# A fused state-space and linear-attention kernel: the data load over two queues, cosines from ScalarE, PSUM reads on either engine, wider lag products, and a new instruction order

## The chip, the core and the metric

The kernel runs on one core of a Trainium2 chip. The time is device microseconds of one execution. Five executions of the kernel before gave 340.03 to 342.0 us, with a median of 341.09 us. Besides, one execution was taken by the hardware profiler, and every row below is from it.

## What is computed

The input x is 2048 positions by 512 channels. The output is `g * a + (1 - g) * b`, where g is a sigmoid gate per position.

Branch a is a long convolution (a state-space model). Each channel d has a kernel K of 2048 lags, the real part of a sum over 128 states n, and `y = irfft(rfft(K) * rfft(x))` per channel, plus a skip term:

```
P = exp(dt * A * l)              # complex, for every channel, state, lag l
K = einsum("dn,dnl,dn->dl", C, P, dt * B).real
```

Branch b is linear attention with 32 heads of 16 features. Queries and keys pass a small matrix and a softmax of both signs, `phi = [softmax(p), softmax(-p)]`; keys and values are summed to one matrix per head, queries are multiplied with it and divided by their sum, and the result is multiplied by `wo`.

## The kernel before

**Plan.** Nothing is scheduled by a compiler. Every piece of work is recorded with `P.add(engine, cost, function, deps, ...)` (class `Plan`, L92). `Plan.schedule` (L161) then places the pieces one by one by their written costs, priorities and buffer rings, and the pieces are emitted in that order. Each engine works through its own queue in order. `TIES` (L97) are seeds of random changes to the priorities; together with the costs they fix the order. A piece may name several engines with a cost each, and the planner takes the one that ends first: the helper `evict` (inside `keys_and_spectrum`) does so for copies from PSUM.

**Loads and tables (`prepare`).** ScalarE's queue issues six parameter loads (L356). SP's queue issues UD (x in 16 pieces of 128 KB, `load_ud` L1426), the weights (`load_w`) and log_dt (`load_ld`, tiles ldc and ld). Tables of sines and cosines for the transform (TB, TI, TJ, W) come from `trig`: POOL writes a ramp into the buffer tgc, VectorE turns it into an integer angle (L397, L398), ScalarE takes the sine. TB has three planes: sine, cosine (both by `trig`) and the negated sine (L414, VectorE). After a table load, a chain over VectorE and ScalarE makes C and D (Ctab, Dtab), from which the powers of the state-space model are made. It starts with dt = exp(log_dt) (tile dtc) and with copies of the transposed B (L491, L492). In between, TensorE transposes x (xT) and makes the spectrum of x (psA, XAu, psB, XU). The gate is `gps`, `gz`, `gT`, and in row form `zps`, `zrow`.

**Keys.** For 16 tiles of positions: pk (TensorE), Ek (two exponentials), Zk (sum), vp, vr (product), kvp (accumulated). Then KVbd, KVT and Mw combine keys, values and wo.

**Queries.** Four blocks: pq, Eq (exponentials), zs (sums), a chain lnZ, den, apm, then aexp and the product Eq (L1046), and bps (16 of them), written to DRAM as bSd.

**Convolution.** For 8 heads of 64 channels, in two chunks each: exponentials E and cosines cs of args (ScalarE; each head needs a change of the activation table and back), the products A (L1102 to L1104) and R (L1116, L1117) on VectorE, kps on TensorE, its copy KD, psA, its copy XA. A transform (`transform`) per two heads, the last two heads singly: psB, copy XK, products t with the spectrum of x, psz, copy Zr, a turn through DRAM (Zd, ZT), psy, the sum bS, four stores. The very last transform takes another way without DRAM (L1276, Z, L1319), and splits its stores over two queues. The eight copies KD, and XA, XK, Zr, are on ScalarE.

R is made one lag part at a time:

```
lo = -x if o == 1 else x                              # ns, L1114
R[:, o, :, 32:64] = E[:, :, 32:64] * x                # L1116, 1024 elements
R[:, o, :, 0:32]  = E[:, :, 0:32] * lo[:, :, ::-1]    # L1117, 1024 elements
```

Of the kernel before, what the change touches and what calls it, by code (L numbers as in the profile page):

```python
# [91 lines left out]
class Plan:  # L92
# [3 lines left out]
    SLACK = 0.0  # L96
    TIES = ((52116, 4, 0.1), (24065, 0.5, 0.1), (41416, 1, 0.1), (45222, 1, 0.05), (61293, 2, 0.02), (71070, 0.5, 0.1),  # L97
            (31770, 1, 0.02), (57566, 0.5, 0.1), (45785, 1, 0.02), (57629, 8, 0.02), (66806, 2, 0.02), (29666, 2, 0.02),
            (61795, 2, 0.1), (13489, 2, 0.05), (14232, 0.5, 0.05), (54586, 0.5, 0.02), (70633, 2, 0.1), (38980, 0.5, 0.05),
            (69021, 4, 0.02), (29818, 2, 0.02), (36790, 2, 0.05), (49753, 1, 0.05), (54801, 2, 0.05), (64205, 4, 0.02),  # L100
            (37415, 2, 0.05), (26019, 0.5, 0.02), (40764, 1, 0.02), (81418, 0.5, 0.02), (60489, 0.5, 0.02), (18238, 0.5, 0.02),
            (76206, 0.5, 0.05), (96767, 4, 0.05), (53026, 0.5, 0.02), (71470, 1, 0.02), (92667, 0.5, 0.05), (83600, 4, 0.02),
            (94213, 4, 0.02), (56684, 4, 0.02), (33149, 8, 0.02), (31465, 2, 0.05), (85177, 2, 0.02), (77498, 1, 0.02),
            (99872, 0.5, 0.02), (5344, 1, 0.05), (71573, 1, 0.02), (46960, 4, 0.02), (29130, 8, 0.02), (30878, 1, 0.05),
            (24195, 2, 0.02), (71220, 0.5, 0.05))
# [27 lines left out]
    def dma(self, busy, late, fn, deps=(), take=(), drop=(), rw=("", ""), move=0.0):  # L133

        i = self.add("SP", busy, fn, deps, take, rw=rw)
        m = self.add("D", move, lambda: None, [i]) if move else i
        n = self.add("W", late, lambda: None, [m], (), drop)
        n.issue = i
        for k in rw[0].split():
            if self.keys[k][1] and i in self.keys[k][1]:  # L140
                self.keys[k][1].append(n)
        for k in rw[1].split():
            self.keys[k] = (n, [])
        return n
# [16 lines left out]
    def schedule(self, bias, slack=0.0):  # L161
# [7 lines left out]
        while left:  # L169
            cand = []  # L170
            for n in left:
                best_e = None
                for e, c in (n.eng if isinstance(n.eng, list) else [(n.eng, n.cost)]):
                    t = free.get(e, 0.0) if e not in "WX" else 0.0
                    for d in n.deps:
                        x = d.end + (self.LAT if d.at != e else 0.0)
                        if x > t:
                            t = x
                    if best_e is None or t + c < best_e[0]:
                        best_e = (t + c, t, e, c)  # L180
                _, t, e, c = best_e
                if n.tab is not None and n.tab != state:
                    continue
                ok, ring = True, None
                for r in n.take:
                    if isinstance(r, str) and r not in self.dyn:
                        continue
                    alt = []
                    for q in ([r] if isinstance(r, str) else r):
                        m = taken[q] - self.k[q]  # L190
                        if q in shut or (m >= 0 and m not in given[q]):
                            continue
                        alt.append((max(t, given[q][m].end + self.LAT if m >= 0 else since[q].end if q in since else 0.0), -self.k[q] + taken[q], q))
                    if not alt:
                        ok = False
                        break
                    t, _, ring = min(alt)
                if ok:
                    cand.append((t, -n.prio - bias[n.i], n.i, n, e, c, ring))
# [37 lines left out]
    def bias(self, seeds):  # L237
        import random
        b = [0.0] * len(self.nodes)
        for s, amp, share in seeds:  # L240
            r = random.Random(s)
            for i in range(len(b)):
# [92 lines left out]
def prepare(P, tc, nc, g, evict, psum):  # L335
# [22 lines left out]
    P.dma(1.1, 3.0, lambda: g.load_ld(), rw=("", "ldc ldb"))  # L358
    P.add("W", 7.0, lambda: None, rw=("raw0", "raw"))
    for tg in range(4):  # L360
        P.dma(4.2, 3.0, lambda tg=tg: g.load_ud(tg), rw=("", f"ud{tg}"))
    P.dma(2.5, 5.5, lambda: g.load_w(), rw=("", "wsm wqk"))
# [4 lines left out]
    def first():  # L367
# [5 lines left out]
        nc.gpsimd.memset(F.mpi[:], -PI_S)  # L373
        F.v = [g.ctmp.tile([128, 2048], I32, name=f"tgv{i}") for i in range(2)]
# [37 lines left out]
    for i, o in ((0, SIN), (1, COS)):  # L412
        trig(lambda i=i: tb(i), 2048, p63, lambda o=o: o, 1, [[2, 32], [128, 64]], f"TB{i}")
    V(1.6, lambda: nc.vector.tensor_scalar(out=tb(2), in0=tb(0), scalar1=-1.0, scalar2=None, op0=ALU.mult), r="TB0", w="TB2")  # L414
# [230 lines left out]
def keys_and_spectrum(P, tc, nc, g, psum):  # L645
# [147 lines left out]
    for s2 in range(8):  # L793
        K = Bag()
        red = []
        for u in range(2):
# [20 lines left out]
            a = P.add("PE", 1.05, pk, [a] if u else [sp, lnexp] + xt + kp, take=["bk"] + ([] if u else ["Ek", "Zk", "vr"]))  # L817
# [9 lines left out]
        for u in range(2):  # L827
# [25 lines left out]
            a = P.add("PE", 1.05, pv, [a], take=["bk"], rw=("wqk", ""))  # L853
            c = P.add("DVE", 1.36, sc, [a, l], drop=["psum"])
            kv = [P.add("PE", 0.45, kn, [c] + kv, drop=(["Ek", "vr"] if u else []))]
# [4 lines left out]
def plan_tables(P, nc, g, psum, h, prev, start=()):  # L860
# [4 lines left out]
    for i in range(2):  # L865
        G = 2 * h + i
        for b2 in range(2):
# [14 lines left out]
            a = P.add("PE", 0.62, pe, [T.first] if b2 else list(start), take=[psq] + (["E"] if b2 == 0 else []))  # L882
# [3 lines left out]
    for i in range(2):  # L886
# [14 lines left out]
        ra.append((P.add("PE", 0.62, pe, T.nE + list(start), take=[psq, "cs"]), sc))  # L901
# [7 lines left out]
def queries_and_convolution(P, tc, nc, g, psum, sh, sp, sl, kv, bank, evict):  # L909
# [3 lines left out]
    W1 = fc.W1[:].rearrange("p r i d -> p (r i d)")  # L913

# [55 lines left out]
    for b in range(4):  # L970
        Q = Bag()
        eq = []
        for m in range(4):
# [14 lines left out]
            a = P.add("PE", 1.0, pq, [sh, sp] + ([a] if m else []), take=["bk"] + ([] if m else ["r8"]))  # L988
# [13 lines left out]
        z = P.add("PE", 2.4, zz, eq + [sk], take=["acc", "nrm"])  # L1002
# [29 lines left out]
        for i in range(4):  # L1032
# [39 lines left out]
            pb = P.add("PE", 2.1, pbm, em + [pb] + mw, take=["bk", "bs"], drop=(["r8", "nrm"] if i == 3 else []))  # L1072
# [9 lines left out]
    def kgen(h, T, XA, new):  # L1082
# [4 lines left out]
        for cc in range(2):  # L1087
# [3 lines left out]
            def Cb(i, d0=d0):  # L1091
                return g.C[:, i, :, d0:d0 + 32].unsqueeze(2).to_broadcast([128, 4, 8, 32])

            def Db(i, d0=d0):
                return g.D[:, i, :, d0:d0 + 32].unsqueeze(1).to_broadcast([128, 4, 8, 32])

            def a_half(o, c=c, Cb=Cb, Db=Db):
# [3 lines left out]
                (i0, j0), (i1, j1), op = (((0, 0), (1, 1), ALU.add), ((0, 1), (1, 0), ALU.subtract))[o]  # L1101
                nc.vector.tensor_tensor(out=c.A[:, o], in0=Cb(i0), in1=Db(j0), op=ALU.mult)  # L1102
                nc.vector.tensor_tensor(out=tmp[:], in0=Cb(i1), in1=Db(j1), op=ALU.mult)  # L1103
                nc.vector.tensor_tensor(out=c.A[:, o], in0=c.A[:, o], in1=tmp[:], op=op)  # L1104

            def r_half(o, c=c, cc=cc):
                if o == 0:
                    c.R = g.rk.tile([128, 2, 32, 64], BF16, name="R")
                E = T.E[cc]
                x = T.cs[cc][:, o]  # L1110
                lo = x
                if o == 1:
                    ns = g.wk.tile([128, 32, 32], BF16, name="ns", tag="tmp", bufs=1)
                    nc.vector.tensor_scalar(out=ns[:], in0=x, scalar1=-1.0, scalar2=None, op0=ALU.mult)  # L1114
                    lo = ns[:]
                nc.vector.tensor_tensor(out=c.R[:, o, :, 32:64], in0=E[:, :, 32:64], in1=x, op=ALU.mult)  # L1116
                nc.vector.tensor_tensor(out=c.R[:, o, :, 0:32], in0=E[:, :, 0:32], in1=lo[:, :, ::-1], op=ALU.mult)  # L1117
                if o == 1:
                    T.E[cc] = T.cs[cc] = None
            a0 = P.add("DVE", 1.95, lambda f=a_half: f(0), [sk], take=["A"])  # L1120
            a1 = P.add("DVE", 1.95, lambda f=a_half: f(1), [a0])
            tdeps = [T.nE[2 * cc], T.nE[2 * cc + 1], T.nc[cc]] if T.nE else []
            r0 = P.add("DVE", 1.3, lambda f=r_half: f(0), tdeps + [sk], take=["R"])
            r1 = P.add("DVE", 1.65, lambda f=r_half: f(1), [r0], drop=["E", "cs"])
# [6 lines left out]
            kps.append(P.add("PE", 1.4, lambda f=kp: f(0), [a0, a1, r0, r1] + kps, take=([psq, "KD"] if cc == 0 else []), drop=["A", "R"]))  # L1131

        def kd():
            K.KD = g.wk.tile([128, 2, 4, 128], BF16, name="KD", bufs=1)
            nc.scalar.copy(out=K.KD[:], in_=K.ps[:].rearrange("p c g e t -> p c g (e t)"))
            K.ps = None
        d = P.add("ACT", 1.03, kd, kps, drop=["psum"])
        for cc in range(2):
# [12 lines left out]
            def ex(cc=cc, box=box):  # L1151
                slot = (0 if new else 2) + cc
                nc.scalar.copy(out=XA.t[:].rearrange("p r i (c d g) -> p (r i) c d g", d=4, g=4)[:, :, slot, :, :],
# [3 lines left out]
            K.done.append(P.add("ACT", 1.03, ex, [s], drop=["psum"]))  # L1157
# [21 lines left out]
    def transform(XA, ready, Q, off, nd, far, L, last):  # L1179
# [11 lines left out]
        for r0 in range(0, 32, ns):  # L1191
# [20 lines left out]
            def xk(box=box):  # L1212
                box.XK = g.fpool.tile([128, ns, nd], BF16, name="XK", tag="XK", bufs=2)
                nc.scalar.copy(out=box.XK[:].rearrange("p s (c e x) -> p (s c) e x", e=2, x=16),  # L1214
# [18 lines left out]
            x = P.add("ACT", 1.03, xk, [b], drop=["psum"])  # L1233
# [14 lines left out]
            def fe(box=box):  # L1248
                box.Z = g.fpool.tile([128, ns, nd], BF16, name="Zr", tag="Zr", bufs=2)
                nc.scalar.copy(out=box.Z[:], in_=box.ps[:])  # L1250
# [6 lines left out]
            zn.append(P.add("ACT", 1.03, fe, [z] + zn[-1:], drop=["psum"]))  # L1257
# [111 lines left out]
def full_kernel(tc, A_u, A_A_re, A_A_im, A_B_re, A_B_im, A_C_re, A_C_im, A_log_dt, A_Dskip,  # L1369
# [7 lines left out]
    with ExitStack() as ctx:  # L1377
# [48 lines left out]
        def load_ud(tg):  # L1426
            for dj in range(4):
                nc.sync.dma_start(out=g.UD[32 * dj:32 * dj + 32, 16 * tg:16 * tg + 16, :],  # L1428
# [130 lines left out]
```

The softmax here doesn't subtract the row's maximum and nothing guards it: scores larger than these inputs give would overflow.

## Time and profile before

| what | value |
|---|---|
| median of 5 runs | 341.09 us |
| profiled execution, its own time | 341.22 us |
| its span | 339.4 us |
| mean granted TensorE clock | 0.827 |
| TensorE, VectorE, ScalarE busy | 247.3, 279.4, 257.2 us |
| DMA | 24.62 MB in 58666 packets, 54145 of them under 512 B |
| first product of the table chain on VectorE (L455) starts | 26.04 us |
| first Ek starts | 80.22 us |
| first and last bps | 153.84 us, 219.4 us |
| last R ends | 305.2 us |

In the rows below, PE is TensorE, DVE is VectorE, ACT is ScalarE, SPq and ACTq are the queues on which DMAs are issued. A row of the timeline has start, duration, engine, line, operation, output and input, and in brackets how long the engine was idle before it and what ended that. A row of the windows has the stretch, and for each engine the busy time with the number of its instructions, then the granted clock, the share of the 16 DMA engines that was busy (transfers overlap, so it can be over 1) and GB/s.

### The profile page before, as it was taken

What the parts mean: (1) busy time and instruction counts of PE and PEld (TensorE: products, weight loads), DVE (VectorE), ACT (ScalarE), POOL (GpSimd) and SP (SyncE); (2) the same over time, 40 slices, a digit from 0 to 9 for tenths busy, and PEclk for the clock granted to TensorE, in tenths of its full rate; (3) what the DMA queues carried; (4) which work ended last, traced back from release to release, by engine and by line L of the source; (5) the groups of instructions that cost most, each with busy time, mean ns of one, the idle gap of its engine ahead of it and who ended that gap; (6) DMA issues with size and microseconds to landing.
All of it is one profiled execution on the core that took longest, in us unless ns stands there. A gap on an engine that the chain in (4) does not pass through costs nothing.

```text
span 339.4 us, 9785 instructions
## 1 busy us (share of the span) xinstructions
PE 247.3 (73%) x4290; PEld 145.8 (43%) x4320; DVE 279.4 (82%) x478; ACT 257.2 (76%) x332; POOL 12.2 (4%) x24
## 2 busy tenths in 40 slices
PE   0417675479998979569999998976776769978750
PEld 0405564355554424233544544444343534456530
DVE  8969999995897985896598897299999999895531
ACT  2847998896977557964976897899979998897200
POOL 5420010000000000000000000000000000000000
PEclk9955569556999978957999999996998985697985
DMA  9991600000000000000201011272176278768444
GB/s 144 249 151 37 150 3 0 2 0 2 2 3 2 4 0 2 2 1 17 49 15 34 17 33 31 46 179 90 64 181 130 68 187 185 191 186 172 113 79 80
DMA packets 58666, 24.62 MB, mean 73 GB/s; under 512 B 54145, under 2 KB 55297, under 8 KB 58113
## 3 DMA queue, kind: packets, MB, share of 16 engines
q1 hardware_dynamic: 54400, 23.10, 30.9%
q10 hardware_dynamic: 4224, 0.92, 1.9%
q8 instruction: 33, 0.54, 0.7%
q14 instruction: 9, 0.07, 0.1%
HBM read 11.42 MB, written 8.39 MB: 58 GB/s over the span
## 4 chain that ended last, share of the span: by engine, by line
DVE 39%; PE 37%; issue 7%; ACT 7%; SPq 5%; DMA 4%; ACTq 0%; DVEq 0%
PE bps L1056 7%; DVE A L1104 5%; DVE Atmp L1103 5%; DVE A L1102 5%; PE pk L803 5%; DVE R L1117 4%; PE pq L981 4%; PE vp L835 4%; SPq L1428 3%; PE args L876 3%; PE aexp L1041 2%; DVE R L1116 2%; PE kps L280 2%; DVE pt L493 2%; DVE t L1221 2%
## 5 line engine op out<-in xcount | busy, mean ns | idle before, releaser
L83 ACT ACTIVATE E<-args 128x1024 bf16<-128x1024 f32 x32 | 32.0, 1037 | 3.5 <-PE args L876 3.5
L1056 PE MATMUL bps<-Mw,Eq 128*128 128x512 bf16 x122 | 31.2, 394 | 1.7 <-DVE Eq L1046 1.1
L83 ACT ACTIVATE cs<-args 128x1024 bf16<-128x1024 f32 x32 | 30.8, 1032 | 0.1
L1046 DVE TENSOR_TENSOR Eq<-Eq,aexp 128x512 bf16<-128x512 bf16 x32 | 20.4, 682 | 10.2 <-PE aexp L1041 10.2
L681 PE MATMUL psA<-W,UD 128*64 128x256 bf16 x128 | 16.8, 420 | 16.1 <-DMA ldc<-in_A_log_dt_dram 5.5
L75 ACT ACT_TABLE_LOAD x20 | 25.7, 1283 | 1.1 <-PEq L1543 0.7
L1116 DVE TENSOR_TENSOR R<-E,cs 128x1024 bf16<-128x1024 bf16 x32 | 21.9, 686 | 4.3 <-PE kps L280 4.3
L876 PE MATMUL args<-selE,stat 64*128 64x512 bf16 x64 | 21.3, 446 | 5.2 <-ACT cs L83 2.9
L280 PE MATMUL kps<-R,A 128*32 128x64 bf16 x1024 | 18.8, 230 | 8.0 <-DVE A L1104 3.9
L815 DVE TENSOR_REDUCE Zk<-Ek 128x64 f32<-128x1024 bf16 x16 | 18.8, 1214 | 6.0 <-ACT Ek L83 5.9
L1104 DVE TENSOR_TENSOR A<-A,Atmp 128x1024 bf16<-128x1024 bf16 x32 | 22.1, 692 | 1.1
L1102 DVE TENSOR_TENSOR A<-Ctab,Dtab 128x1024 bf16<-128x1024 bf16 x32 | 21.9, 686 | 1.2 <-PE kps L280 1.2
L83 ACT ACTIVATE Ek<-pk 128x512 bf16<-128x512 f32 x32 | 16.8, 599 | 7.9 <-PE pk L803 7.9
L280 PEld LDWEIGHTS <-A 128*32 128x32 bf16 x1024 | 17.1, 152 | 11.8 <-issue 6.7
L1103 DVE TENSOR_TENSOR Atmp<-Ctab,Dtab 128x1024 bf16<-128x1024 bf16 x32 | 21.9, 685 | 0.0
L681 PEld LDWEIGHTS <-UD 128*64 128x64 bf16 x128 | 13.1, 207 | 19.5 <-issue 19.0
L1244 PE MATMUL psz<-t,TI 128*128 128x512 bf16 x50 | 17.8, 464 | 4.4 <-ACT cs L83 3.0
L595 PE MATMUL xps<-ident,UD 128*128 128x128 bf16 x64 | 7.2, 286 | 18.8 <-DMA Dcol_b<-in_A_Dskip_dram 10.9
L839 DVE TENSOR_TENSOR vr<-vp,vr 128x512 bf16<-128x512 f32 x32 | 19.6, 681 | 0.0
L83 ACT ACTIVATE Eq<-pq 128x512 bf16<-128x512 f32 x32 | 16.8, 612 | 3.5 <-PE pq L981 3.5
L1056 PEld LDWEIGHTS <-Eq 128*128 128x128 bf16 x128 | 12.0, 100 | 16.9 <-DVE Eq L1046 3.0
L1214 ACT CAST XK<-psB 128x1024 bf16<-128x1024 f32 x16 | 16.1, 1025 | 1.6 <-PE psB L1206 0.9
(195 smaller groups left out, 560.8 us busy)
## 6 DMA issues: line engine op xcount, KB each, us to landing
XUs<-XU SPq DMA_DIRECT2D x8, 512.0 KB, 6.7
Zd<-Zr SPq DMA_DIRECT2D x14, 256.0 KB, 4.5
ZT<-Zd SPq DMA_DIRECT2D x6, 512.0 KB, 5.6
UD<-in_A_u_dram SPq DMA_DIRECT2D x16, 128.0 KB, 5.3
bSd<-bs SPq DMA_DIRECT2D x16, 128.0 KB, 1.9
bS<-bSd SPq DMA_DIRECT2D x4, 512.0 KB, 7.9
out_dram<-bS SPq DMA_DIRECT2D x30, 64.0 KB, 2.4
wqk<-in_B_wqkv_dram SPq DMA_DIRECT2D x1, 1024.0 KB, 6.6
```

The source lines that it names most:

```text
L75: p = self.nc.scalar.preload_act_table_set(name)
L83: i = self.nc.scalar.activation(**kw)
L280: nc.tensor.matmul(kps[32 * dj:32 * dj + 32, g4, e, :], lhsT=A[:, ri, :, :, d].rearrange("p a b -> p (a b)"), rhs=R[:, ri, d, :], start=(r ...
L681: nc.tensor.matmul(box.ps[64 * e:64 * e + 64, i, :], lhsT=g.UD[:].rearrange("p t (e g) -> p g e t", e=2)[:, gw * h + 4 * g4 + i, e, :], rh ...
L839: nc.vector.tensor_tensor(out=K.v[:, u, sg, :, 0:32].rearrange("p m (h e) -> p m h e", e=16), in0=box.ps[:].rearrange("p (m h e) -> p m h ...
L876: nc.tensor.matmul(box.ps[:, 8 * j:8 * j + 8, :], lhsT=g.stat[0:64, G, :], rhs=g.selE[0:64, d0:d0 + 8, :], start=True, stop=True, tile_pos ...
L1046: nc.vector.tensor_tensor(out=e, in0=e, in1=box.ps[:], op=ALU.mult)
L1056: nc.tensor.matmul(box.ps[:], lhsT=Q.e[:, m, sg, 128 * i:128 * i + 128], rhs=g.Mw[:, 4 * sg + m, :], start=(k == 0), stop=False, skip_grou ...
L1102: nc.vector.tensor_tensor(out=c.A[:, o], in0=Cb(i0), in1=Db(j0), op=ALU.mult)
L1103: nc.vector.tensor_tensor(out=tmp[:], in0=Cb(i1), in1=Db(j1), op=ALU.mult)
L1104: nc.vector.tensor_tensor(out=c.A[:, o], in0=c.A[:, o], in1=tmp[:], op=op)
L1116: nc.vector.tensor_tensor(out=c.R[:, o, :, 32:64], in0=E[:, :, 32:64], in1=x, op=ALU.mult)
```

## The change

- `load_ud` may go on SP or on ScalarE's queue, as the planner chooses. In the built order, one of the four groups (four DMAs) is on ScalarE's, ahead of the first table. SP issues the weights first, then log_dt, then the other twelve pieces of UD.
- TB's cosine is made by ScalarE from the integer angle of the sine: an Abs into tgc, then a sine of it; the negated sine is a third activation. The second angle on VectorE and POOL and the negation L414 go.
- KD, XA, XK, Zr may be copied by ScalarE or VectorE; a new constant (LEAN, 0.6) is added to VectorE's end in that choice. In the built order VectorE has one XA and two XK; KVT, which had the choice before, is on ScalarE.
- R of both lag parts is one product of 2048 elements, twice per chunk, with the negation made in place between them.
- Some costs are changed, SLACK is 0.1, and TIES are 300 new seeds with ranges. The order is another one all over: the gate follows the keys, selE follows the last vr, lnZ and apm of the first block precede the first change of the activation table.

The core of the diff (TIES and the remaining costs left out):

```diff
-    P.dma(1.1, 3.0, lambda: g.load_ld(), rw=("", "ldc ldb"))
+    ld = P.dma(1.7, 3.0, lambda: g.load_ld(), rw=("", "ldc ldb")).issue
...
-        P.dma(4.2, 3.0, lambda tg=tg: g.load_ud(tg), rw=("", f"ud{tg}"))
-    P.dma(2.5, 5.5, lambda: g.load_w(), rw=("", "wsm wqk"))
+        P.dma(3.3, 2.5, lambda tg=tg: g.load_ud(tg, nc.scalar if P.cur.at == "ACT" else nc.sync), [ld], rw=("", f"ud{tg}"), eng=[("SP", 3.3), ("ACT", 3.4)], move=1.5)
+    P.dma(3.5, 5.5, lambda: g.load_w(), rw=("", "wsm wqk"), move=4.0)
...
-    for i, o in ((0, SIN), (1, COS)):
-        trig(lambda i=i: tb(i), 2048, p63, lambda o=o: o, 1, [[2, 32], [128, 64]], f"TB{i}")
-    V(1.6, lambda: nc.vector.tensor_scalar(out=tb(2), in0=tb(0), scalar1=-1.0, scalar2=None, op0=ALU.mult), r="TB0", w="TB2")
+    trig(lambda: tb(0), 2048, p63, lambda: SIN, 1, [[2, 32], [128, 64]], "TB0")
+    k0, v0, f0 = f"v{(nv[0] - 1) % 2}", (nv[0] - 1) % 2, 2.0 * PI_S / 8192.0
+    S(2.0, lambda: nc.scalar.activation(out=F.col[:], in_=F.v[v0][:], func=ACT.Abs, scale=f0, bias=F.mpi[:]), r=k0, w="col")
+    S(2.0, lambda: act(out=tb(1), in_=F.col[:], func=ACT.Sin, scale=-1.0, bias=HALF_PI), r="act col", w="TB1")
+    S(2.0, lambda: act(out=tb(2), in_=F.v[v0][:], func=ACT.Sin, scale=-f0, bias=F.ppi[:]), r="act " + k0, w="TB2")
...
+    def copy(out, in_):
+        if P.cur.at == "DVE":
+            nc.vector.tensor_copy(out=out, in_=in_)
+        else:
+            nc.scalar.copy(out=out, in_=in_)
...
-                nc.vector.tensor_tensor(out=c.R[:, o, :, 32:64], in0=E[:, :, 32:64], in1=x, op=ALU.mult)
-                nc.vector.tensor_tensor(out=c.R[:, o, :, 0:32], in0=E[:, :, 0:32], in1=lo[:, :, ::-1], op=ALU.mult)
...
+                    nc.vector.tensor_tensor(out=c.R[:, :, :, 32:64], in0=E[:, :, 32:64].unsqueeze(1).to_broadcast([128, 2, 32, 32]), in1=x[:], op=ALU.mult)
+                    nc.vector.tensor_scalar(out=x[:, 1], in0=x[:, 1], scalar1=-1.0, scalar2=None, op0=ALU.mult)
+                else:
+                    nc.vector.tensor_tensor(out=c.R[:, :, :, 0:32], in0=E[:, :, 0:32].unsqueeze(1).to_broadcast([128, 2, 32, 32]), in1=x[:, :, :, ::-1],
+                                            op=ALU.mult)
...
-            x = P.add("ACT", 1.03, xk, [b], drop=["psum"])
+            x = P.add([("ACT", 1.03), ("DVE", 1.24)], 1.03, xk, [b], drop=["psum"])
```

## The prediction

> **What bounds the kernel now.** I read the page's busy shares, then its slices, then windows of 20 us, because shares of a whole span mix stages.
>
> ```profile
> span 339.4 us, 9785 instructions
> PE 247.3 (73%) x4290; PEld 145.8 (43%) x4320; DVE 279.4 (82%) x478; ACT 257.2 (76%) x332; POOL 12.2 (4%) x24
> ...
> DMA  9991600000000000000201011272176278768444
> ```
>
> No engine is full over the span; the first three DMA slices are. The windows (engine busy, granted clock, DMA share, GB/s) show a stage with its own limit each time:
>
> ```profile
> 40.00:60.00 20.00, 12.17 (x185) 10.40 (x185) 19.65 (x34) 19.11 (x23) 0.95 (x1) 0.76 0.00 1
> ...
> 160.00:180.00 20.00, 19.79 (x225) 9.74 (x227) 16.20 (x28) 17.29 (x25) 0.00 (x0) 1.00 0.16 34
> 180.00:200.00 20.00, 19.43 (x311) 10.68 (x313) 17.91 (x31) 16.05 (x25) 0.00 (x0) 1.00 0.10 22
> ...
> 240.00:260.00 20.00, 12.37 (x262) 7.32 (x264) 19.76 (x34) 18.13 (x20) 0.00 (x0) 0.99 0.46 122
> ```
>
> From 26 to 76 us VectorE and ScalarE are both full (tables of the SSM kernel); from 155 to 219 TensorE is (queries, bps); from 221 to 305 VectorE is (products of the lags). What starts the first of these is in the timeline:
>
> ```profile
> 6.02 0.40 SPq L1433 DMA_DIRECT2D wc<-in_B_w_phi_dram  x1
> ...
> 9.88 11.03 SPq L1428 DMA_DIRECT2D UD<-in_A_u_dram  x12
> ...
> 20.96 0.71 SPq L1423 DMA_DIRECT2D ldc<-in_A_log_dt_dram  x1
> ...
> 25.80 0.21 ACT L83 ACTIVATE dtc<-ldc 128x4 f32<-128x4 bf16 x1 [2.13 <-DMA ldc<-in_A_log_dt_dram]
> ...
> 26.04 0.69 DVE L455 SCALAR_TENSOR_TENSOR pt<-Are,dtc 128x512 f32<-128x512 bf16 x1 [3.21 <-ACT dtc L83]
> ```
>
> log_dt is issued last, and VectorE waits 3.2 us for it. The SP queue's own waits say why issuing takes so long:
>
> ```profile
> SPq L1433 <- DMA Aim<-in_A_A_im_dram: 1.0, 1, 1.0
> ```
>
> wc has nothing to do with A_im: the built program gives every DMA one of eight semaphores in turn, and an issue waits until the transfer eight places earlier has landed.
>
> **Step 1, the start: +6.2 us.** The change moves ldc and ld ahead of UD, so that wait of 3.2 us goes. Next is late what ScalarE must do before its copies of B and C: it gains an Abs and two sines and loses one sine of 2048 (2.00 us each, so +4.0), while VectorE loses 1.28, 2.25 and 1.66 us. Four UD issues now stand on ScalarE's queue, ahead of all of that. In the built order they wait for Bim, Wv, ldc and the first UD that SP issues; that one stands behind ld, which waits for wqk. Params and wqk together are 1.8 MB; at the 181 to 381 GB/s of the windows around that time wqk lands near 9, ld is issued, UD at about 10, and lands 3.4 us later at the earliest (UD's landings: 3.4 to 7.2). Queued behind these waits are the Abs, the sines, an xT eviction and the table load; VectorE's products and TensorE's psA groups wait for those. So ScalarE is free for the Abs at about 13.4; the integers it needs are ready at about 9. Behind it come: Abs and cosine 4.05; on POOL the next ramp, which now waits for the cosine since both use one buffer (1.14), and the small ramp (1.17); VectorE's W, TI group 1.8 and the next integers 0.85; the third ramp 1.6 on POOL before masks and selectors (2.6); TJ and integers 2.0; the last sine 1.15, table load 1.28, copy 0.6, with gaps of 0.6: 18.8. VectorE's first product starts at 32.2 instead of 26.04. The bounds: +1.9 if nothing waits for landings, +12 if UD lands late. From there to the last table VectorE is busy 49.1 of 50.4 us and both orders put 10 evictions on it and 20 on ScalarE: the delay passes on whole. [...] With the DMA share at 1.4 from 4 to 24 us the data doesn't end earlier either.
>
> **Step 2, no gate between tables and keys: -2.3.** Before, the gate's 64 matmuls and two XU groups stand in TensorE's queue ahead of pk:
>
> ```profile
> 74.70 1.85 PE L763 MATMUL gps<-gw,xT 128*128 128x1 bf16 x64 [0.29 <-ACT XAu L662]
> ...
> 78.70 5.13 PE L803 MATMUL pk<-Wkp,xT 128*128 128x512 bf16 x15 [0.33 <-issue]
> ...
> 80.22 1.09 ACT L83 ACTIVATE Ek<-pk 128x512 bf16<-128x512 f32 x2 [0.80 <-PE pk L803]
> ```
>
> The last sine of the tables ended 6.5 us before that Ek. In the new order only two evictions (1.9), the table load (1.28) and one eviction (0.95) lie between: 4.2. Bounds 0 and -2.5.
>
> **Step 3, keys: -2.9.** selE (2.29), its helpers and zrow (0.68) leave VectorE's queue ahead of the last Zk and vr; it was full from 110 to 126. They reappear behind the last vr, where it waited 3.1 us for kvp anyway. TensorE's matmuls there differ by about nothing (gate and two groups in, 8 args and zps out). Bounds 0 and -4.
>
> **Step 4, keys to queries: +1.5, then -3.8.** KVT goes to ScalarE behind twelve Eq exponentials, and gate and zrow go between KVbd and Mw: +1.5 (0 to 3). From the last Mw (139.4) to the first bps (153.84) the old order has a table load, four cs and a table load (1.28, 3.77, 1.28) ahead of lnZ on ScalarE. The new one puts lnZ, den and apm ahead of them, behind five E (1.03) and three A groups (1.93) at most: 10.9 instead of 14.7. Bounds -1 and -6.
>
> **Step 5, queries: +3.** Between first and last bps the new order has 128 kps and 8 args more: 2 x 1.06 (64 kps took 1.06 at full clock) and 8 x 0.23 make 4.0. TensorE idled 2.3 us in that stretch, some of which covers it. Bounds 0 and +5.
>
> **Step 6, the VectorE stage.** Counted in both orders, what VectorE has left after the last Eq is the same: 20 groups of A, R for 10 chunks, 32 t, 8 bS. But before, it stood still first, its two R buffers full (R waited 4.3 for kps, in one wait); with one head more of kps done, that goes: -4.3 (0 at worst). "Either engine" moves one XA and two XK to VectorE, just here: 3 x 1.22 = +3.7 (+2 if ScalarE's ends waited). ScalarE's relief is off the path. The wider R:
>
> ```profile
> 302.36 0.69 DVE L1116 TENSOR_TENSOR R<-E,cs 128x1024 bf16<-128x1024 bf16 x1
> ...
> 302.96 0.69 DVE L1117 TENSOR_TENSOR R<-E,cs 128x1024 bf16<-128x1024 bf16 x1
> ...
> 303.57 0.42 DVE L1114 TENSOR_SCALAR ns<-cs 128x1024 bf16<-128x1024 bf16 x1
> ...
> 303.90 0.69 DVE L1116 TENSOR_TENSOR R<-E,cs 128x1024 bf16<-128x1024 bf16 x1
> ...
> 304.50 0.69 DVE L1117 TENSOR_TENSOR R<-E,ns 128x1024 bf16<-128x1024 bf16 x1
> ```
>
> Two products become one, 32 fewer. [...] Against it the negation now feeds the very next product, 0.42 instead of its 0.33: 16 x 0.09. I take -1 (0 to -5).
>
> **Step 7, the end: -2.5.** Before, the last bS is a far one at 330.70, then four stores on SP, issued until 336.9. Now the near half comes last, its stores split over SP and ScalarE. Bounds -4 and +1: twelve stores stand ahead of the last ZT on SP.
>
> Sum: 6.2 - 2.3 - 2.9 + 1.5 - 3.8 + 3.0 - 4.3 + 3.7 - 1.0 - 2.5 = **-2.4**. The profiled run took 341.2 (1.8 outside its span), the median is 341.1: **338.7 us**.
>
> **Rivals.** (a) Landings don't hold ScalarE: its first UD wait ends at 8 and the Abs starts with its integers at 9. Step 1 falls to +1.9: 334.4. For it: parameters landed in under 5 us; against: Wv can't land before wqk. Chance 0.15. (b) Slower: the same queue holds ScalarE longer. The other steps return 8.6, so the end turns when the first product starts after 34.6, the Abs after 15.8. If the UD that is waited for takes 7.2 and its issue comes at 11.4, the Abs starts at 19.3, the product at 38.1: +12 - 8.6 gives 344.5. For it: the DMA engines are full then. Chance 0.30, with returns that fail me counted here. (c) The change moves nothing: work left to VectorE after the last Eq is equal, the new order only reshuffles, and 341 stays: 0.13. The likeliest case, 335.5 to 340, has 0.42.
>
> **Numbers.** A measurement here can tell 0.3% (1.0 us) from no change. Faster takes the likeliest case and (a), 0.57; same 0.13; slower 0.30. The likeliest case's own range is 335.5 to 340; to hold 8 in 10 the range goes from 331 to 346.
>
> **What the profile after would show.** UD issues on ScalarE's queue ending near 13 and the Abs right behind; VectorE's first pt near 32; first Ek near 84; first bps 11 us after Mw; no wait of R for kps; last R near 304 to 306; R at 1.2 us each. I am wrong if the Abs starts at 9 or after 16, if VectorE idles between 221 and 305 shifted, or if TensorE waits for Eq in the queries.

## The result, and the profile after

The changed kernel took 342.31 us (median of 43 runs), the kernel before 340.56 us (median of 80 runs beside them). The ratio is 1.004, with a 95% interval from 1.002 to 1.006: slower by about 1.4 us, where 338.7 us and a gain of 2.4 had been forecast. The medians count every execution; the ratio, here and below, leaves out those more than 1.5% above the fastest of the same kernel, which is why it shows less than the medians do. The profiled execution took 342.04 us with a span of 340.3, 0.9 more than the span before. (One correction to the list of changes: TIES holds 513 seeds, not 300. No step rests on it.)

The page of the changed kernel, the three rows that answer to those of before:

```profile
span 340.3 us, 9745 instructions
...
PE 244.5 (72%) x4288; PEld 143.6 (42%) x4320; DVE 274.9 (81%) x445; ACT 259.3 (76%) x332; POOL 7.9 (2%) x24
...
DMA  7990260000000000000111011237168386989564
```

VectorE does 4.5 us less work and the kernel is not faster. The windows show the same stages as before, and in each the engine that was full is full again:

```profile
40.00:60.00 20.00, 12.21 (x169) 10.75 (x168) 19.69 (x34) 19.62 (x28) 1.25 (x3) 0.83 0.29 67
...
180.00:200.00 20.00, 19.26 (x208) 9.47 (x208) 13.61 (x23) 17.64 (x28) 0.00 (x0) 1.00 0.13 28
...
240.00:260.00 20.00, 14.81 (x262) 8.47 (x263) 19.74 (x30) 19.33 (x21) 0.00 (x0) 0.76 0.44 118
```

The new thing is in the first 35 us. From the timeline:

```profile
4.43 0.37 SPq L1541 DMA_DIRECT2D Wv<-in_B_wqkv_dram  x1
...
10.41 0.35 SPq L1528 DMA_DIRECT2D ld<-in_A_log_dt_dram  x1
10.66 5.65 ACTq L1532 DMA_DIRECT2D UD<-in_A_u_dram  x4
10.81 11.34 SPq L1532 DMA_DIRECT2D UD<-in_A_u_dram  x12
15.99 0.32 ACTq L1532 DMA_DIRECT2D UD<-in_A_u_dram  x1
16.41 2.00 ACT L514 ACTIVATE tgc<-tgv,mpi 128x2048 f32<-128x2048 int32 x1 [9.51 <-DMA UD<-in_A_u_dram]
...
34.12 0.22 ACT L83 ACTIVATE dtc<-ldc 128x4 f32<-128x4 bf16 x1
...
34.99 0.68 DVE L557 SCALAR_TENSOR_TENSOR pt<-Are,dtc 128x512 f32<-128x512 bf16 x1
```

ScalarE stands idle for 9.51 us in front of the Abs, and the bracket names what ended that: a landing of UD. The rows above it say why: ld is issued only at 10.41 (SP's own waits put 4.2 us of that down to wqk), UD behind it, and ScalarE's four issues last until 16.31. In windows of 0.2 us the four appear one by one, at 10.66, 12.68, 13.22 and 15.99 (the row of 15.99 is from there, and is part of the row of four above it). Each starts when an earlier load lands, on the semaphore of that load (107, 101, 103 and 105 in the trace, of the eight from 100 to 107 that the loads take in turn): Bim, issued at 2.43, took 8.2 us; Wv, at 4.43, 8.2; ldc, at 4.84, 8.4; SP's first UD, at 10.81, 5.2. These are the four that the prediction had named. VectorE's first product with dt, at 26.04 before, comes at 34.99.

Now the same places of the program in three profiled executions: before, after, and the first experiment below (after, with all of UD on SP). The last two columns are the shift against before. Each kernel is read from one execution, and executions of the kernel before lie between 337.17 and 342.48 us: a shift of 1 us in this table says something only where rows name its cause.

| place | before | after | UD on SP | after | UD on SP |
|---|---|---|---|---|---|
| first VectorE product with dt starts | 26.04 | 34.99 | 25.78 | +8.95 | -0.26 |
| last sine of the tables ends | 73.75 | 82.49 | 73.28 | +8.74 | -0.47 |
| first Ek starts | 80.22 | 87.02 | 78.12 | +6.80 | -2.10 |
| zj (after the last kvp) starts | 129.39 | 132.45 | 124.68 | +3.06 | -4.71 |
| last Mw ends | 139.44 | 142.22 | 134.46 | +2.78 | -4.98 |
| first bps starts | 153.84 | 152.52 | 144.75 | -1.32 | -9.09 |
| last Eq ends | 216.69 | 220.24 | 211.45 | +3.55 | -5.24 |
| last R ends | 305.19 | 309.73 | 300.69 | +4.54 | -4.50 |
| span | 339.4 | 340.3 | 331.8 | +0.9 | -7.6 |

So the change loses 8.7 us in the start and gets 7.8 back over the remaining 258.

One thing moves beside the change. In the first 17.5 us from the first bps, the granted clock was 0.90 before and 0.74 after; with UD on SP, in the same order of instructions, it was 0.90 again.

### The profile page after: what moved, and what is told of

It reads as the page before. It is cut to its first block, busy times and chain, and to the rows that moved or that the text cites. A ratio compares the mean times of both kernels' runs of the same rounds, so it can differ in the third digit from the quotient of the medians.

```text
span 340.3 us, 9745 instructions
## 1 busy us (share of the span) xinstructions
PE 244.5 (72%) x4288; PEld 143.6 (42%) x4320; DVE 274.9 (81%) x445; ACT 259.3 (76%) x332; POOL 7.9 (2%) x24
## 5 line engine op out<-in xcount | busy, mean ns | idle before, releaser
L1165 PE MATMUL bps<-Mw,Eq 128*128 128x512 bf16 x120 | 32.4, 406 | 4.2 <-DVE Eq L1155 3.6
L783 PE MATMUL psA<-W,UD 128*64 128x256 bf16 x128 | 15.2, 393 | 24.5 <-ACT pt L594 14.2
L917 DVE TENSOR_REDUCE Zk<-Ek 128x64 f32<-128x1024 bf16 x16 | 18.6, 1213 | 5.6 <-ACT Ek L83 5.5
L377 PE MATMUL kps<-R,A 128*32 128x64 bf16 x1024 | 17.8, 234 | 7.2 <-DVE R L1221 5.7
L377 PEld LDWEIGHTS <-A 128*32 128x32 bf16 x1024 | 16.4, 152 | 11.8 <-issue 7.6
L1310 PE MATMUL psB<-XA,TB 64*128 64x64 bf16 (+1 forms) x640 | 15.1, 205 | 7.7 <-DVE bS L1432 3.1
L1218 DVE TENSOR_TENSOR R<-E,cs 128x2048 bf16<-128x2048 bf16 x16 | 19.5, 1219 | 0.0
L1221 DVE TENSOR_TENSOR R<-E,cs 128x2048 bf16<-128x2048 bf16 x16 | 19.3, 1221 | 0.2
```

What stands on the lines that cost most here:

```text
L377: nc.tensor.matmul(kps[32 * dj:32 * dj + 32, g4, e, :], lhsT=A[:, ri, :, :, d].rearrange("p a b -> p (a b)"), rhs=R[:, ri, d, :], start=(r ...
L783: nc.tensor.matmul(box.ps[64 * e:64 * e + 64, i, :], lhsT=g.UD[:].rearrange("p t (e g) -> p g e t", e=2)[:, gw * h + 4 * g4 + i, e, :], rh ...
L1165: nc.tensor.matmul(box.ps[:], lhsT=Q.e[:, m, sg, 128 * i:128 * i + 128], rhs=g.Mw[:, 4 * sg + m, :], start=(k == 0), stop=False, skip_grou ...
L1218: nc.vector.tensor_tensor(out=c.R[:, :, :, 32:64], in0=E[:, :, 32:64].unsqueeze(1).to_broadcast([128, 2, 32, 32]), in1=x[:], op=ALU.mult)
```

## The experiments

**All of UD on SP.** The order of every engine stays that of the changed kernel; only the four issues leave ScalarE's queue.

```diff
-g.load_ud(tg, nc.scalar if P.cur.at == "ACT" else nc.sync)
+g.load_ud(tg, nc.sync)
```

> The changed kernel in its own order, with all sixteen pieces of UD issued by SP; ScalarE's queue keeps only its six parameter loads. Theory H (ScalarE's queue is held by the four UD issues, and the start's delay reaches the end): the Abs starts near 7.2 instead of 16.41, as soon as its integers are ready; dtc near 25 to 27 instead of 34.12; last sine of the tables near 74 to 76 instead of 82.49; the time 6 to 9 us less than the changed kernel's, about 334 to 336, or 0.98 of the kernel before. Rival L (the later stages have limits of their own, and the start's delay is made good there anyway): the front moves as above, but the time falls by 2 us or less. Rival D (the data is late on any queue, and the spectrum of x waits for it): the front moves, the first Ek does not move by more than 3 us.

332.97 us, ratio to before 0.980 (0.976 to 0.985). Its timeline:

```profile
7.20 2.00 ACT L514 ACTIVATE tgc<-tgv,mpi 128x2048 f32<-128x2048 int32 x1 [0.34 <-DVE tgv L497]
...
9.49 0.35 SPq L1528 DMA_DIRECT2D ld<-in_A_log_dt_dram  x1
...
9.88 11.85 SPq L1532 DMA_DIRECT2D UD<-in_A_u_dram  x16
...
24.91 0.22 ACT L83 ACTIVATE dtc<-ldc 128x4 f32<-128x4 bf16 x1
```

The Abs waits for its integers alone; the Abs, dtc, the first product with dt and the last table sine are each 9.21 us earlier than after. 8.5 of these reach the end. On the way it is not one number: at the first bps 7.77 are left, and the queries, from there to the last Eq, take 66.7 us instead of 67.7, at the higher clock (0.90 in their first 17.5 us, there 0.74). UD itself is no later: SP issues all sixteen pieces in 11.85 us, the twelve alone took 11.34. Theory H holds; L and D fall.

**The same four issues on ScalarE, three sines later.** This separates the queue from the place in it.

```diff
+u = next(n for n in order if n.i == 11)       # the UD group on ScalarE
+order.remove(u)
+order.insert(1 + next(i for i, n in enumerate(order) if n.i == 33), u)   # behind TB's last sine
```

> The changed kernel in its own order, with the same four UD issues on ScalarE's queue, but behind the three sines of TB and ahead of the first sine of TJ. Theory H (it is the wait of the issues for earlier landings that costs, not that ScalarE issues): the Abs starts at 7.2; behind the sines, from about 15.2, the four issues go without a wait and take about 2 us, some of it in the time in which ScalarE waited for VectorE's integers anyway; dtc within 0 to 2 us of its 24.91 of the run with all of UD on SP, and the time at most 2 us above that run's 333. Rival Q (a second queue that moves data costs ScalarE as such, wherever it stands, through the queue or through contention): the time stays at 338 or more.

332.89 us, ratio 0.980 (0.975 to 0.986), dtc at 24.91 again. (The profiled execution took 336.07 us; only its first 25 us are read here.) The issues still held the first sine of TJ (17.86 instead of 15.81), but the second one waits for VectorE until 21.49 in both, so that cost is hidden. In this kernel ScalarE may issue, if it does not issue ahead of work that others wait for. Rival Q falls.

**The weights last.** Does ScalarE wait for wqk, or for UD?

```diff
+u = next(n for n in order if n.i == 17)       # the five weight loads
+order.remove(u)
+order.insert(1 + next(i for i, n in enumerate(order) if n.i == 5), u)    # behind UD on SP
```

> The changed kernel in its own order, with its four UD issues in their place on ScalarE's queue ahead of the Abs, and the five weight loads moved behind UD on SP. It asks what the four issues waited for. Theory W (for transfers behind wqk, 1 MB, which held ld and through it the first UD): ScalarE's last UD issue comes at 9 to 12 us instead of 16, the Abs at 9.5 to 12.5; if the masks on VectorE then don't wait for the late weights, dtc is at 27 to 30 instead of 34.12 and the time at 335 to 338. Rival U (for UD transfers themselves, which are slow while 2 MB of them are in flight): the Abs stays at 14.5 or later. If the masks wait for the weights instead, the Abs moves as in W, but dtc stays at 31 or later, and the time at 339 or more.

341.23 us, ratio 1.000 (0.997 to 1.003). From its timeline:

```profile
7.77 0.34 ACTq L1535 DMA_DIRECT2D UD<-in_A_u_dram  x1
...
10.95 3.44 ACTq L1535 DMA_DIRECT2D UD<-in_A_u_dram  x3
14.49 2.00 ACT L517 ACTIVATE tgc<-tgv,mpi 128x2048 f32<-128x2048 int32 x1 [6.22 <-DMA UD<-in_A_u_dram]
```

The Abs comes 1.92 us earlier, not 4 to 7. Of the 9.21 us, 1.92 go with the weights ahead and 7.29 stay. The four issues start at 7.77, 10.95, 11.75 and 14.07; the last of them waits for SP's third UD, issued at 8.72, and the bracket names UD again. The parameter loads, now beside UD, took no less time to land than in the changed kernel (Bim 8.5 us, there 8.2). That is rival U, at 14.49 against its bound of 14.5. dtc (32.20) and the last table sine are 1.92 earlier too, and the ratio is 0.004 below that of the changed kernel, about 1.4 us, though their intervals overlap.

**Without the Abs.** What do the new cosines cost?

```diff
-nc.scalar.activation(out=F.col[:], in_=F.v[v0][:], func=ACT.Abs, scale=f0, bias=F.mpi[:])
-act(out=tb(1), in_=F.col[:], func=ACT.Sin, scale=-1.0, bias=HALF_PI)
+act(out=tb(1), in_=F.v[v0][:], func=ACT.Sin, scale=f0, bias=F.mpi[:])
```

> The changed kernel in its own order, all of UD on SP, with the Abs of TB's cosine left out (the cosine plane then holds a second sine, so the kernel leaves out that part of the computation). It asks what the new cosine costs. Theory C (the Abs and the ramp of TJ that waits behind the cosine stand on the chain to dtc, as the prediction's step 1 put them): dtc 2.0 us earlier than 24.91, at about 22.9, or earlier by up to 2.6, since the ramp needs no buffer back either. What follows behind it gave back 1.0 of 2.25 us in the run with the constants moved, so the time is 1 to 2 us below 332.97. Rival M (the chain waits for VectorE's masks and for the xT eviction, which hides the Abs): dtc moves by less than 0.7 us, the time by less than 0.7.

330.18 us, ratio 0.971 (0.966 to 0.975). dtc is at 22.35, 2.56 earlier: theory C. The last table sine is 1.70 earlier, the median 2.8 lower; part of the latter arises in the queries (first bps 2.44 earlier, last Eq 4.23, at like clocks of 0.91 and 0.90), for which this run gives no cause. What stops the front from moving further is in the rows: an eviction of xT, whose xps (at 16.95) waits 2.61 us for UD.

```profile
18.02 1.01 ACT L764 CAST xT<-xps 128x1024 bf16<-128x1024 f32 x1 [3.03 <-PE xps L697]
...
22.35 0.22 ACT L83 ACTIVATE dtc<-ldc 128x4 f32<-128x4 bf16 x1
```

**log_dt first, in the kernel before.** The half of the new load that was to remove the wait of 3.2 us.

```diff
+order.remove(self.ld)                          # the two log_dt loads
+order.insert(min(i for i, n in enumerate(order) if n.eng == "SP"), self.ld)
```

> The kernel before in its own order, with the two log_dt loads moved ahead of UD and the weights on SP. Theory H (the delay of the table chain reaches the end, in this kernel too): VectorE's first product starts at about 23.9 instead of 26.04, as ScalarE had waited 2.13 us for ldc, and the time falls by about 2 us, to 338 to 339. Rival L (the later stages make it good anyway): the product moves, the time stays within 0.7 us. Rival N (something else is late at once, such as the copies of the transposed B): the product itself moves by less than 1 us.

343.21 us, ratio 1.009 (1.005 to 1.012): slower than the kernel before. dtc is no longer waited for, and comes 1.90 us later, with two more loads ahead of UD: ScalarE's queue is held by an eviction of xT (at 20.31 in the kernel before, where its xps had waited 4.54 us for UD):

```profile
24.33 1.01 ACT L664 CAST xT<-xps 128x1024 bf16<-128x1024 f32 x1 [3.83 <-PE xps L597]
```

None of the three theories has it slower. Rival N comes nearest (something else is late at once), but names the copies of B, not xT, and no loss. The delay of 1.90 is there, at 1.5 to 1.9, at every place of the table above, and the last bS is 1.89 later: in this kernel too, and in these two executions, what the start loses the end loses.

**Constants later.** On the version with UD on SP, the masks and selectors leave VectorE's queue ahead of the second TJ integers.

```diff
+u = next(n for n in order if n.i == 146)      # masks and selectors
+order.remove(u)
+order.insert(1 + next(i for i, n in enumerate(order) if n.i == 53), u)   # behind the integers
```

> The changed kernel in its own order, all of UD on SP, and the masks and selectors (2.6 us of VectorE, ahead of the second TJ integers) moved behind these integers. Theory H (a delay or gain of the table chain's start reaches the end whole): the second TJ sine starts near 19.0 instead of 21.50, dtc near 22.4 instead of 24.91, and the time is 2 to 2.6 us below that of the run with all of UD on SP (332.97): about 330.6, ratio 0.973. Rival L (the chain's start is no longer what counts once UD is off ScalarE's queue): the chain moves, the time stays within 0.7 us of 333. Rival X (an xT eviction that waits for UD takes the place of the integers in ScalarE's queue): dtc moves by less than 1 us.

331.94 us, ratio 0.979 (0.974 to 0.984). dtc comes at 22.66, 2.25 earlier, but the last table sine only 1.31 earlier: the products of the tables wait 0.43 and 0.33 for ScalarE, and ScalarE stands idle 4.38 us before an XAu (1.53 without the move). Yet zj and the first bps are 2.63 and 2.64 earlier, so the keys give back what the tables had lost. It is the queries that lose: from the first bps to the last Eq they take 67.8 us instead of 66.7, at a granted clock of 0.74 instead of 0.90 in their first 17.5 us. The span is 1.3 shorter. Of times alone, 331.94 and 332.97 can't be told apart. H is right as far as the first bps, and about half of it reaches the end.

**The copies back on ScalarE.** On the changed kernel, one XA and two XK.

```diff
-        if P.cur.at == "DVE":
-            nc.vector.tensor_copy(out=out, in_=in_)
-        else:
-            nc.scalar.copy(out=out, in_=in_)
+        nc.scalar.copy(out=out, in_=in_)
```

> The changed kernel in its own order, with the one XA and two XK that VectorE copies returned to ScalarE. Theory V (VectorE bounds the stretch after the last Eq, so its 3.6 us of copies there are paid in full): 2.5 to 3.6 us less than the changed kernel, about 339. Rival S (ScalarE is as full there, 19.33 of 20 us, and the copies of 1.0 us each push E and cs back, for which R waits): within 1 us of the changed kernel. Theory H of the start says nothing on this run.

342.65 us, ratio 1.007 (1.004 to 1.010). No gain: V falls, and the time is S's. Its reason is only near: not R waits for E and cs, but t for XK. VectorE, less 3.6 us of copies, waits instead. Its waits between 219 and 310 us:

```profile
DVE t L1325 <- ACT XK L1019: 2.7, 2, 2.0
DVE A L1209 <- PE kps L377: 2.1, 1, 2.1
```

The first of these does not occur in the changed kernel in this stretch. From the last Eq to the last R it is 88.4 us instead of 89.5, a gain of 1.1; from there to the end of the last bS it is 28.7 instead of 26.2, and the last bS starts 1.7 later. What lengthens the end was not traced.

**R narrow.** On the changed kernel.

```diff
-R[:, :, :, 32:64] = E[:, :, 32:64] (to both k) * x            # 2048 elements, likewise 0:32
+for k in range(2): R[:, k, :, 32:64] = E[:, :, 32:64] * x[:, k]    # 1024 each, likewise 0:32
```

> The changed kernel in its own order, with each wide R product of 2048 elements split into two of 1024. By the rows of the changed kernel (a wide one takes 1.196 us to the next start, two narrow ones took 2 x 0.602 in the kernel before) the width saves 0.01 each: within 0.7 us of the changed kernel. [...]

343.05 us, ratio 1.011 (1.007 to 1.015); the last R ends 0.92 later, the last bS 1.00 later. 0.45 of this is there at the last Eq; 0.47 arises in the VectorE stage. Between the last Eq and the last R a pair of narrow products takes 1.262 us from start to start of the next, a wide one 1.196; the negation takes 0.344 there, and 0.402 on average in the changed kernel (0.461 where the wide product that needs its result follows at once). 20 x 0.066 - 10 x 0.058 = 0.7 us. For the width alone my reading ahead of the run, 0.01 each, was wrong: it saves 0.066.

But this run keeps the negation in place, which the kernel before did not have, so it does not undo the whole step. Against the kernel before there is no gain. Rows of the changed kernel:

```profile
306.78 1.22 DVE L1218 TENSOR_TENSOR R<-E,cs 128x2048 bf16<-128x2048 bf16 x1
308.04 0.43 DVE L1219 TENSOR_SCALAR cs<-cs 128x1024 bf16<-128x1024 bf16 x1
308.50 1.23 DVE L1221 TENSOR_TENSOR R<-E,cs 128x2048 bf16<-128x2048 bf16 x1
309.64 0.68 DVE L1325 TENSOR_TENSOR t<-XU,XK 128x1024 bf16<-128x1024 bf16 x1
```

The product ahead of the negation, which reads what the negation overwrites, takes 1.25 to the next start; the other takes 1.14, from 308.50 to 309.64. Per chunk, products and negation take 1.253 + 0.402 + 1.138 = 2.79 us. Before, with the negated copy in a buffer of its own, they took 4 x 0.602 + 0.336 = 2.74 us. Over the ten chunks of the stage the change costs 0.5 us.

**ZT ahead of the stores.** On the version with UD on SP, twelve output stores moved behind the last far transform's loads.

```diff
+for k in (926, 819, 814):                      # three stores of four DMAs each
+    u = next(n for n in order if n.i == k)
+    order.remove(u)
+    order.insert(1 + next(i for i, n in enumerate(order) if n.i == 974), u)  # behind ZT
```

> The changed kernel in its own order, all of UD on SP, and on SP's queue near the end the twelve output stores that stood ahead of the last far transform's turn through DRAM moved behind its two ZT loads. Theory Z (the chain that ended last ran over these stores: 5.4 us of ZT landing after an issue at 323.12, behind four stores): ZT is issued 2 to 5 us earlier and the last products of that transform start with it; the time falls by 1.5 to 2.5 us against the run with all of UD on SP, to about 331, as far as the near half's Z (ready at 328.86 in the changed kernel) lets it. Rival N (the near half's own path, psz, Z and psy, ends at the same time): within 0.7 us of 333. Rival W (the stores themselves end last when they are put later): slower by 1 us or more.

340.21 us, ratio 1.003 (1.000 to 1.006): 7 us slower than without the move. From its timeline:

```profile
312.16 1.89 SPq L1371 DMA_DIRECT2D ZT<-Zd  x2
...
314.10 22.00 SPq L1444 DMA_DIRECT2D out_dram<-bS  x22
...
326.13 1.22 DVE L1438 TENSOR_TENSOR bS<-psy,gT 128x1024 bf16<-128x1024 f32 x1 [2.53 <-PE psy L1427]
...
327.39 0.67 ACTq L1444 DMA_DIRECT2D out_dram<-bS  x1
...
329.61 0.32 SPq L1444 DMA_DIRECT2D out_dram<-bS  x1
```

ZT is issued 2.3 us earlier (314.42 with UD on SP), and the last bS ends where it did (327.35 against 327.43): the near half's own path ends it, as rival N has it. But SP issues stores until 336.1, and the span ends at 338.5. The row of 22 hides a gap, which the last two rows, from windows of 0.1 us, and SP's own waits show:

```profile
SPq L1444 <- DMA out_dram<-bS: 4.7, 1, 4.7
```

Eleven stores are issued by 324.91; the twelfth waits until 329.61 for another output store to land. ScalarE's first store of the near half, issued at 327.39, took 2.2 us to land, so it lands at that moment. Both stores have the same one of the eight semaphores (105), as a load and the one it waited for had at the start. So stores that were ready now wait for one that can go only after the last bS. Issuing itself is not slow: the median of the 22 issues is 0.47 us, and 0.48 with UD on SP. N says why nothing is gained, W why 7 us are lost.

**All three moves.**

> All three moves together on the changed kernel: UD on SP, masks and selectors behind the TJ integers, ZT ahead of the stores. If theories H and Z hold, the gains add, as the first is at the start and the other at the end: about 329 (332.97 less 2.5 and 1.5 to 2), ratio 0.966 to 0.97. If either rival L or N holds, about 331; if W, 332 or more.

338.37 us, ratio 0.996 (0.993 to 0.999). The last bS is 3.2 us earlier than with UD on SP alone, and the span, 335.3, is again the stores': SP waits 4.7 us here too, until 326.47, and ScalarE's first store of the near half, issued at 324.25, lands then. Rival W again. Of the versions that compute the output in full, the one with UD on SP and the constants later is lowest, 331.94 us. It beats both kernels; from the one with UD on SP alone its time can't be told.

## Why the prediction was wrong

The sum was -2.4 and the measured spans give +0.9. By its own steps, with the last Eq as the end of step 5, the measured sizes being differences of the shifts in the table:

| step | predicted | measured |
|---|---|---|
| 1 start | +6.2 | +8.7 |
| 2 no gate between tables and keys | -2.3 | -1.9 |
| 3 keys | -2.9 | -3.7 |
| 4 keys to queries | +1.5, -3.8 | -0.3, -4.1 |
| 5 queries | +3.0 | +4.9 |
| 6 VectorE stage | -4.3 + 3.7 - 1.0 = -1.6 | +1.0 |
| 7 end | -2.5 | -3.6 |
| sum | -2.4 | +0.9 |

Three terms failed: step 1 by size (2.5 us too good), step 5 by size (1.9), and step 6 partly by mechanism (2.6). Steps 2 to 4 gave back 10.0 us where 7.5 stood. That was luck: at the first bps the forecast stood at -1.3 and the measured shift is -1.32, with an error in step 1 and its opposite behind it. The loss against the forecast arises in steps 5 and 6.

**Step 1 failed by size.** The mechanism is as written: issues on ScalarE's queue wait for earlier transfers, and Abs, sines and copies stand behind them. "ScalarE is free for the Abs at about 13.4" was 16.41. Two terms were small: ld and UD were issued at 10.4 and 10.8 where 9 and 10 stood, as wqk took 8.1 us to land; and UD's landing was put at 3.4 us, "at the earliest", where the first UD took 5.2. I had the span 3.4 to 7.2 before me, with a median of 5.3, and took its lower end for the sum. 10.8 and 5.2 give 16.0, where ScalarE's last issue starts. What followed was nearly right: from the Abs it was 17.4 us to VectorE's first product of the chain (at 33.78, the one with the copies of B) and 18.6 to the first with dt, where 18.8 stood. The integers were ready at 7.2, not 9, so the issues cost 9.2, not 4.4.

That an issue also waits for a landing, as the row with wc has it (1.0 us), was read rightly. The runs say when it counts: behind the sines the four issues cost nothing at dtc (24.91 in both), ahead of them 9.2. Wv landed behind wqk, as rival (a) had it against itself: at 12.66, wqk at 10.40 (15.91 and 14.21 before). Nor did the data end earlier: the last piece of UD landed at 26.13, at 25.59 before.

**Rival (b) is what happened,** small: its mechanism, its place and its point of decision. The Abs was to start after 15.8 for the time to rise; it started at 16.41. It had 0.30, and the case with the low landing had 0.42. That the time turned just past this point is in part chance, as steps 2 to 7 returned 7.8, not 8.6. Nor was "nothing moves" right, though the time says almost that: two shifts of 8 us cancel. The run with UD on SP shows the second alone: with the start within 0.3 us of before, everything else gives -7.6 (8.6 was forecast to come back).

**Step 5** was 1.9 short in the table, which ends it at the last Eq. Between its own ends, the first and the last bps, it took 73.4 us against 66.0: +7.3, past its bound of +5. TensorE stood idle no longer (2.4 us against 2.6); it was busy 7.5 longer. By lines, kps cost 1.9 more where 2.1 stood, args 3.8 where 1.8 stood, and bps and aexp, as many as before, 1.9 more for which nothing stood. The granted clock of the whole stretch was 0.94 against 0.97, that of its first 17.5 us 0.74 against 0.90; the forecast had no term for a lower clock. In versions with the changed kernel's order of queries, first bps to last Eq took 67.7 to 68.2 us where that clock was 0.73 or 0.74 (five executions) and 64.8 to 66.7 where it was 0.85 to 0.92 (five). Why the clock differs is open.

**Step 6** was 2.6 too good. R's wait for kps went, as said, but a wait of VectorE for kps stands in its place, at an A. The wait in the kernel before, as the list of waits has it, and the row of the changed kernel:

```profile
DVE R L1116 <- PE kps L280: 4.3, 1, 4.3
...
222.39 0.69 DVE L1209 TENSOR_TENSOR A<-Ctab,Dtab 128x1024 bf16<-128x1024 bf16 x1 [2.15 <-PE kps L377]
```

The prediction had the two buffers of R full; those of A may be full now, which no run tests. Between the last Eq and the last R, VectorE's idle time fell from 6.1 to 3.6 us, by 2.5 and not by 4.3. Its work grew by 3.5, not by 2.7: the three copies cost 3.6, as forecast, and R with its negation costs 0.5 more where -1.0 stood, because the negation in place was charged 0.09 per chunk and holds up the product ahead of it as well; t and bS in the stretch make up the rest. No run shows the saving per instruction that the -1.0 starts from. With R narrow beside it, a wide product came out 0.066 us below two narrow ones, 0.13 per chunk; the negation in place took back 0.07 by itself and 0.12 in the product ahead of it. That the stage would be 3.6 shorter without the copies falls too: with them on ScalarE it is 1.1 shorter, as VectorE waits for ScalarE.

**Steps 2, 3, 4 and 7** hold within 1.8 us, and in sign but for KVT and the gate between keys and queries, which cost nothing where +1.5 stood. (Step 4 has 14.7 us from the last Mw to the first bps before; the two places it names are 14.4 apart.) The end is where a stated sign failed in detail: twelve stores ahead of ZT were called a cost; moved behind it they cost more.

Not settled: how much of the -7.6 each move of the order gives by itself. The moves share buffers and were not undone one by one; the table only says where the time is.

## What to carry to other kernels

The DMAs issued from ScalarE's own queue were a wait in ScalarE's program here, until the last of the transfers landed that their issues waited for: 5.65 us for the four, and the Abs behind them 9.2 later than without. Look at what stands behind an issue, and at what waits for that. Where a chain runs through full stages, most of a shift at its start can arrive at the end: 9.2 us at 7 us became 8.5 at 332. When an unknown landing weighs on the sum, put the median of such landings in, not the earliest: 5.3 for 3.4 would have made the forecast -0.5. And compare a forecast place by place: here an error of 2.5 was hidden at the first bps by its opposite.

## What was not expected of the hardware

An issue waited for a transfer on another queue: SP's twelfth store waited 4.7 us for a store that ScalarE had issued. The granted clock in the first 17.5 us of the queries was 0.74 or 0.90 for one order of TensorE's work. A load placed first made its own user later: log_dt ahead of UD delayed dtc by 1.90 us. From start to start a wide product cost 0.066 us less than two narrow ones; and an in-place negation behind a product added 0.12 to it, which is more.
